# Rests of K and V formed on VectorE instead of GpSimd, and the slope product folded into the row maximum, in an attention and two-expert-layer kernel on one core

## The chip, the core and the metric

The kernel runs on one core of one Trainium2 chip. The metric is device time of that core in microseconds (us), lower is better. PE is TensorE, DVE VectorE, ACT ScalarE, POOL GpSimd, and SP the engine whose queue issues nearly all DMAs here.

## The reference

Three layers follow one another: attention with a window of 128 and a linear bias per head, a gated layer without a nonlinearity, and a routed layer of 8 experts, one per token. All inputs and the output are float32 (the weights of the gated layer arrive as float64).

```python
# attention: batch 4, 8 heads, 576 positions, 64 per head
scores = q @ k.T / sqrt(64)
scores = where((0 <= rel) & (rel < 128), scores + slopes[h] * -abs(rel), -1e9)   # slopes[h] = 2 ** -(h + 1)
scores = scores - max(scores)
attn = exp(scores); attn = attn / (sum(attn) + 1e-9)
x = attn @ v                                  # 2304 tokens x 512
# gated layer
x = ((x @ w_a) * (x @ w_b)) @ w_out           # 512 -> 1536 -> 512
# routed layer
e_idx = argmax(x @ w_gate + modality_bias[modality_id])
out[t] = gate_w[t] * (relu(x[t] @ w1[e]) @ w2[e])   # e = e_idx[t], 512 -> 1024 -> 512
```

## The kernel before

The 2304 tokens are 18 tiles of 128 rows, in seven chunks of 3, 2, 2, 3, 3, 3 and 2 tiles. For each chunk c a loop over j = 0 to 11 runs the gated layer on PE: `mm_ab` twice (tiles ps_ab, L507), the product of the two (gf, L1001 in chunk 0 and L1067 later) and its split into a rounded part and a rest (g, L1006 and L1007, later L1070 and L1071), and `mm_out` (acc, L521). Between these steps stands the attention of the next chunk: an item is one tile of one pair of heads, 72 items in all; those of chunk 0 come first, in a prologue whose order is written out by hand.

PE multiplies in a reduced form of float32 (F32R). To keep precision most operands are split in two: a part rounded by ACT, and the rest, which is the operand minus that part. For chunks 2 to 6 `a_prep_k` makes the rounded part of K on ACT (L192, from tile kr, that a DMA fills at L171) and the rest on POOL (L193, into the second half of tile kk): 20 instructions, 8 of 128x768 and 12 of 128x1024 elements. For chunks 1 to 6 `a_prep_v` does the same with V (L226 on ACT, L227 on POOL, from vr filled at L179, into vv): 24 instructions, 12 of 128x384 and 12 of 128x512. kr and vr have one buffer each, so the load of the next pair's K or V waits in SP's queue until this subtraction has read the tile.

An item's scores run so. PE makes ps_s (L244 or L248). DVE folds the two key tiles into one (`score_sel`, L256), then for each of two heads adds the mask and takes the row maximum in one instruction that also writes p (`score_max`, L262; an instruction that writes the accumulated maximum to mx follows each), then multiplies the two maxima by minus the slopes (`score_neg`, L267, 128x2 elements, from the constant tile nslope). ACT takes the exponential with that product as bias and the slope as scale (`score_exp`, L276). DVE adds 1e-9 to the sums and inverts them (L280, L285). PE turns p (L306, ps_p), ACT and DVE split it (pc, L317 and L318), POOL picks the two triangles out of pc with two affine selects (pt, L320 and L322), and PE multiplies by V (L343 in chunk 0, L378 later).

In chunk 0's loop DVE also takes apart the float64 weights: three bit operations for each half of w_a and w_b and for w_out (f64f, L438, L442, L446), and the rest of the split (wab and wo, L454). In chunk 1 and later it also does the dot products of the router (L588).

Only the prologue has a fixed order. Elsewhere the scheduler puts instructions in order by a simulated time line and priorities; preparation, scores and products of the attention have high priority. Each engine works through its own queue in that order, and an instruction that waits holds up what stands behind it.

Of the kernel before, what the change touches and what calls it, by code (L numbers as in the profile page):

```python
# [7 lines left out]
F32 = mybir.dt.float32  # L8
# [6 lines left out]
ALU = mybir.AluOpType  # L15
PSUM = bass.MemoryType.PSUM
P = 128
# [4 lines left out]
def attn_moe_moe2(ctx: ExitStack, tc, q, k, v, moe_w_a, moe_w_b, moe_w_out, modality_id,  # L22
                  w_gate, w_gate_t, modality_bias, w1, w2, out):
    nc = tc.nc
# [3 lines left out]
    H, D, S = HEADS, DM // HEADS, SEQ  # L28
# [43 lines left out]
    const = ctx.enter_context(tc.tile_pool(name="const", bufs=1))  # L72
# [43 lines left out]
    def mask_of(i):  # L116
        r = (P * i) % S
        if r == 0:
            return masks["first"]
        if S - r < P:  # L120
            assert S - r == HB
            return masks["strad"]
        if r < P:
            assert r == HB
            return masks["after"]
        return masks["base"]

    nslope = const.tile([P, H], F32, name="nslope")
    qscale = const.tile([P, NP], F32, name="qscale")
    RG = N + 3 * P  # L130
    UT = 3 * P
# [51 lines left out]
    def qq_zero(a):  # L183
        for h in range(2):
            nc.gpsimd.memset(a.qq[64 - 64 * h:128 - 64 * h, h, :], 0.0)

    def a_prep_k(a):
# [4 lines left out]
        nc.scalar.copy(out=a.kk[:, :, 0, :n], in_=a.kr[:, :, :n])  # L192
        (nc.gpsimd if KLP else nc.vector).tensor_tensor(out=a.kk[:, :, 1, :n], in0=a.kr[:, :, :n], in1=a.kk[:, :, 0, :n], op=ALU.subtract)  # L193

# [24 lines left out]
    def a_prep_v(a):  # L219
        nk = a.nt + 1  # L220
        if a.c in V32:
            a.vv = a.vr
            return
        a.vv = at.tile([P, MT + 1, 2, 2, D], F32R, tag="vv", bufs=2, name="vv")
        if a.c in V6:
            nc.scalar.copy(out=a.vv[:, :nk, 0], in_=a.vr[:, :nk])  # L226
            nc.gpsimd.tensor_tensor(out=a.vv[:, :nk, 1], in0=a.vr[:, :nk], in1=a.vv[:, :nk, 0], op=ALU.subtract)  # L227
            return
        nc.scalar.copy(out=a.vv[:, :nk, :, 0, :], in_=a.vr[:, :nk])
        nc.gpsimd.tensor_tensor(out=a.vv[:, :nk, :, 1, :], in0=a.vr[:, :nk], in1=a.vv[:, :nk, :, 0, :], op=ALU.subtract)  # L230
# [21 lines left out]
    def score_sel(it):  # L252
        a = it.a
        it.p = at.tile([P, 2, P], F32, tag="p", bufs=3, name="p")
        it.mx = at.tile([P, 8], F32, tag="mx", bufs=4, name="mx")
        nc.vector.copy_predicated(out=it.ps[:, :, P:2 * P], mask=upper.unsqueeze(1).to_broadcast([P, 2, P]), data=it.ps[:, :, 0:P])  # L256

    def score_max(it):
        a = it.a
        m = mask_of(C0[a.c] + it.t)  # L260
        for h in range(2):
            nc.vector.tensor_tensor_reduce(out=it.p[:, h, :], in0=it.ps[:, h, P:2 * P], in1=m, scale=1.0,  # L262
                                           scalar=-3.0e38, op0=ALU.add, op1=ALU.max, accum_out=it.mx[:, h:h + 1])

    def score_neg(it):
        a = it.a
        nc.vector.tensor_tensor(out=it.mx[:, 2:4], in0=it.mx[:, 0:2], in1=nslope[:, 2 * a.hp:2 * a.hp + 2], op=ALU.mult)  # L267

    def score_red(it):
        score_sel(it)  # L270
        score_max(it)
        score_neg(it)

    def score_exp(it):
        for h in range(2):
            nc.scalar.activation(out=it.p[:, h, :], in_=it.p[:, h, :], func=AF.Exp, bias=it.mx[:, 2 + h:3 + h],  # L276
                                 scale=2.0 ** -(2 * it.a.hp + h + 1), accum_out=it.mx[:, 4 + h:5 + h])

    def score_inv(it, rec=True):
        nc.vector.tensor_scalar(out=it.mx[:, 4:6], in0=it.mx[:, 4:6], scalar1=1e-9, scalar2=None, op0=ALU.add)  # L280
        if rec:
            score_rec(it)

    def score_rec(it):
        nc.vector.reciprocal(out=it.mx[:, 6:8], in_=it.mx[:, 4:6])  # L285

    def score_nrm(it):
# [44 lines left out]
    def new_xr(c):  # L332
        xr_t[c] = m1.tile([P, 2, KD, MT * P], F32R, tag="xr", bufs=1, name=f"xr{c}")
# [305 lines left out]
    @hp  # L639
    def a_loads(g):  # L640
        while pos["load"] < len(plist) and first[plist[pos["load"]]] <= g:
            c, hp = plist[pos["load"]]
            pairs[c, hp] = a_load(c, hp)
            pos["load"] += 1

    @hp
    def a_preps(g):
        while pos["prep"] < len(plist) and first[plist[pos["prep"]]] <= g:
            a = pairs[plist[pos["prep"]]]
            a_prep_k(a)  # L650
            a_prep_q(a)
            a_prep_v(a)
            pos["prep"] += 1
# [17 lines left out]
    n0 = NP * CH[0]  # L671
# [76 lines left out]
    with tc.manual_schedule():  # L748
        if WU:
            wz = m1.tile([P, 2 * P], BF16, tag="asb", bufs=2, name="wz")  # L750
            nc.vector.memset(wz.bitcast(F32), 0.0)
            wps = ps_at.tile([P, 2 * P], F32, tag="att", name="ps_w")
            for _ in range(WU):
                nc.tensor.matmul(wps, lhsT=wz[:, 0:P], rhs=wz, start=True, stop=True)
        for h in range(H):
            nc.vector.memset(qscale[64 * (h % 2):64 * (h % 2) + 64, h // 2:h // 2 + 1], 0.125 * 2.0 ** (h + 1))
        new_xr(0)
        a_loads(n0 - 1)
        qq_zero(pairs[0, 0])
        make_masks(lambda: a_preps(0))  # L760
        for h in range(H):
            nc.vector.memset(nslope[:, h:h + 1], -(2.0 ** -(h + 1)))
        for hp_ in range(1, NP):
            qq_zero(pairs[0, hp_])
        consts_load()
        wab_load(0)
        wo_load(0)
        wab_load(1)
        a_loads(n0)
        wo_load(1)  # L770
        wab_load(2)
        wab_load(3)
        for j in range(NCV):
            conv += wab_jobs(j)
            if j == 0:
                conv += wo_jobs(0)

        def st(lim, f, g, *x):
            if 0 <= g < lim:
                f(live[g], *x)  # L780

        def st_s(g):
            if 0 <= g < n0 + 2:
                c, hp, t = items[g]
                live[g] = score_mm(pairs[c, hp], t)

        def conv_step(g):
            if g >= CVS and conv:
                kd = conv[0][0]
                for _ in range(2 if kd == "s" else 1):  # L790
                    if conv and conv[0][0] == kd:
                        conv.pop(0)[1]()

        ns = n0 + 2
        for g in range(-SK, n0):
            st(n0, pt_tr, g)
            st(n0, pv_mm, g - 1)
            st(n0, pv_tr, g - 2)
            if g + SK <= n0:
                st_s(g + SK)  # L800
            r = g + SK - 1
            if r <= n0:
                st(ns, score_sel, r)
            st(n0, pv_x, g - 3, 1)
            if r <= n0:
                st(ns, score_max, r)
            st(ns, score_inv, g, False)
            if r <= n0:
                st(ns, score_neg, r)
            st(ns, score_rec, g)  # L810
            st(n0, pt_cp, g)
            st(ns, score_exp, g + 1)
            conv_step(g)
            st(n0, pv_ev, g - 1)
            st(n0, pv_x, g - 2, 0)
            if CV2 and g >= CV2:
                conv_step(g)
            if g >= -1 and (g + PRP) % CH[0] == 0 and g < n0 - CH[0]:
                a_preps(g + PRP + CH[0])
            if g == CAP - SK:  # L820
                consts_ap()
            if g == CA:
                consts_ad()
            if g == CJ:
                consts_b()
        l1, l2, i0 = (live[n0 + k] for k in (-1, -2, 0))
        pv_x(live[n0 - 3], 1)
        pv_mm(l1)
        pv_tr(l2)
        pv_ev(l1)  # L830
        mm_ab(0, 0, 0, 0)
        pv_x(l2, 0)
        pv_x(l2, 1)
        pv_tr(l1)
        pv_x(l1, 0)
        pv_x(l1, 1)
        st_s(n0 + 1)
        i1 = live[n0 + 1]
        score_red(i1)
        score_inv(i0)  # L840
        score_nrm(i0)
        pt_tr(i0)
        score_exp(i1)
        pt_cp(i0)
        score_inv(i1)
        score_nrm(i1)
# [175 lines left out]
    for c in range(NC):  # L1022
        n = CH[c] * P
        for j in range(NJ):
            if c + 1 < NC:
                b0, n1 = NP * C0[c + 1], NP * CH[c + 1]
                g = b0 + LEAD + min(n1, ((j + 1) * n1 + NJD - 1) // NJD)
            else:
                g = len(items) + 2
# [109 lines left out]
    for a, _ in zip(AE, evac_out(NC - 1)):  # L1139
# [10 lines left out]
                            op0=ALU.subtract, op1=ALU.subtract)  # L1150
# [24 lines left out]
    for o, w_, key, src in ((0, NBIG, 4, sm_f[:NS, 1:2]), (NBIG, NBIG, 4, u_[:, 13:14]),  # L1175
                            (SE, NSML, 12, sm_f[:NS, 1:2]), (SO, NSML, 12, u_[:, 14:15])):
        nc.vector.tensor_scalar(out=vt[:NS, o:o + w_], in0=iot[:NS, 0:w_], scalar1=u_[:, key:key + 1], scalar2=src,
                                op0=ALU.is_equal, op1=ALU.mult)
# [139 lines left out]
```

## Time and profile before

| | before |
|---|---|
| median of 3 runs | 883.31 us (881.21 to 883.39) |
| the profiled execution | 884.64 us, of which 882.9 us are the span from the first to the last instruction |
| busy in the span: PE | 826.9 us (94%) |
| DVE | 593.0 us (67%) |
| ACT | 435.8 us (49%) |
| POOL | 256.3 us (29%) |
| mean granted TensorE clock | 0.971 of full speed |

Busy time is the union of an engine's instructions. An instruction that the hardware holds up after it has begun counts as busy while it stands. The granted clock is 1.0 at 2.4 GHz and 0.5 at 1.2 GHz, so a mean between them is a share of either.

### The profile page before, as it was taken

How to read it: one execution, taken by the hardware profiler on the slowest of the kernel's cores; microseconds unless marked ns; L12 is line 12 of the kernel's file. 1: busy time of each engine (PE TensorE's matmuls, PEld its weight loads, DVE VectorE, ACT ScalarE, POOL GpSimd, SP SyncE). 2: the span in 40 equal slices, each digit the busy share in tenths (PEclk: the TensorE clock that was granted, in tenths of full speed). 3: DMA queues.
4: the chain of work that ended last, by engine and by line, in shares of the span. 5: the costliest groups of instructions: out<-in, count | busy, mean ns of one | idle time of the engine just before them, and what ended most of it. 6: DMA issues, size and time to landing. Idle time of an engine off the chain costs nothing.

```text
span 882.9 us, 14476 instructions
## 1 busy us (share of the span) xinstructions
PE 826.9 (94%) x4806; PEld 752.4 (85%) x4806; DVE 593.0 (67%) x1771; ACT 435.8 (49%) x1156; POOL 256.3 (29%) x289
## 2 busy tenths in 40 slices
PE   7899786989989999999999999999999999989994
PEld 5788775879888998998989999999988998978893
DVE  6999999897697779656965586358375444545420
ACT  5746464753765765656446552242245444454420
POOL 5412243342354534442334221100133120132011
PEclk9889898999999999999999999999999999998998
DMA  9993333478867455542454235547438654566201
GB/s 273 353 397 127 111 128 117 154 198 248 183 180 192 137 164 179 152 116 91 142 160 132 81 109 167 153 146 234 95 117 293 202 192 125 177 209 214 69 37 39
DMA packets 66276, 145.52 MB, mean 165 GB/s; under 512 B 11951, under 2 KB 32079, under 8 KB 66192
## 3 DMA queue, kind: packets, MB, share of 16 engines
q1 hardware_dynamic: 62576, 134.64, 50.0%
q0 software_dynamic: 3616, 9.86, 3.0%
q8 instruction: 40, 0.66, 0.3%
q14 instruction: 44, 0.36, 0.1%
HBM read 125.63 MB, written 19.11 MB: 164 GB/s over the span
## 4 chain that ended last, share of the span: by engine, by line
PE 43%; issue 24%; DVE 20%; POOL 4%; DMA 4%; ACT 3%; SPq 1%; POOLq 0%; ACTq 0%; DVEq 0%
PE ps_ab L507 24%; PE acc L521 11%; PE ps_o L378 3%; DVE junk L588 3%; DVE f64f L442 2%; DVE f64f L446 2%; POOL out L1109 2%; DMA wgt<-in_wgt 2%; POOL xg L909 2%; DVE qq L216 2%; PE ps_s L248 2%; DVE wab L454 1%; DVE p L262 1%; DVE f64f L438 1%; DVE ps_s L256 1%
## 5 line engine op out<-in xcount | busy, mean ns | idle before, releaser
L507 PE MATMUL ps_ab<-xr,wab 128*128 128x384 f32 (+1 forms) x2016 | 348.3, 321 | 21.6 <-ACT wab L453 5.9
L507 PEld LDWEIGHTS ps_ab<-xr,wab 128*128 128x128 f32 x2016 | 317.2, 192 | 35.0 <-ACT wab L453 9.7
L521 PE MATMUL acc<-wo,g 128*128 128x512 f32 x648 | 173.3, 400 | 1.0 <-DVE sc L553 0.8
L521 PEld LDWEIGHTS acc<-wo,g 128*128 128x128 f32 x648 | 116.4, 189 | 21.1 <-DVE g L1071 1.2
L1102 PE MATMUL ps_y<-w2s,h 128*128 128x512 f32 x456 | 112.2, 400 | 0.8 <-ACT h L1232 0.8
L320 POOL TENSOR_SCALAR_AFFINE_SELECT pt<-pc 128x512 fp32r<-128x512 f32 (+1 forms) x72 | 51.3, 713 | 194.7 <-DVE pc L318 111.2
L588 DVE CUSTOM_DVE_ANT_0 junk<-x,wgt 128x512 f32<-128x512 f32 x128 | 100.7, 786 | 8.2 <-DMA wgt<-in_wgt 4.4
L1119 PE MATMUL ps_h<-xT,w1s 128*128 128x384 f32 x576 | 103.2, 336 | 0.0
L1102 PEld LDWEIGHTS ps_y<-w2s,h 128*128 128x128 f32 x456 | 85.5, 191 | 18.3 <-ACT h L1232 1.0
L1119 PEld LDWEIGHTS ps_h<-xT,w1s 128*128 128x128 f32 x576 | 99.7, 188 | 1.1 <-issue 0.5
L276 ACT ACTIVATE p<-p,mx 128x128 f32<-128x128 f32 x144 | 56.7, 395 | 48.0 <-DVE mx L267 47.6
L1109 POOL DMA_INDIRECT out<-y,idx x19 | 22.3, 1171 | 166.2 <-ACT y L1108 165.0
L1070 ACT CAST g<-gf 128x256 fp32r<-128x256 f32 (+1 forms) x72 | 33.0, 459 | 62.9 <-DVE gf L1067 61.2
L193 POOL TENSOR_TENSOR kk<-kr,kk 128x1024 fp32r<-128x1024 f32 (+1 forms) x20 | 45.3, 2263 | 58.4 <-ACT kk L192 58.0
L1067 DVE TENSOR_TENSOR gf<-ps_ab,asb 128x256 f32<-128x256 f32 (+1 forms) x72 | 35.0, 486 | 40.4 <-PE ps_ab L507 31.0
L378 PE MATMUL ps_o<-pt,vv 128*128 128x256 f32 x360 | 57.2, 293 | 4.4 <-POOL pt L320 2.4
L876 DVE TENSOR_TENSOR w2s<-wr,w2s 128x1024 fp32r<-128x1024 f32 x24 | 29.3, 1225 | 43.1 <-ACT w2s L875 42.8
L378 PEld LDWEIGHTS ps_o<-pt,vv 128*128 128x128 f32 x360 | 49.9, 191 | 7.2 <-POOL pt L320 3.2
L322 POOL TENSOR_SCALAR_AFFINE_SELECT pt<-pc 128x512 fp32r<-128x512 f32 (+1 forms) x72 | 54.3, 754 | 0.0
L1063 ACT COPY asb<-ps_ab 128x256 f32<-128x256 f32 (+1 forms) x72 | 30.4, 422 | 48.4 <-PE ps_ab L507 47.1
L293 ACT ACTIVATE p<-p,mx 128x128 f32<-128x128 f32 x120 | 41.4, 394 | 25.1 <-DVE mx L285 24.2
L1123 DVE SCALAR_TENSOR_TENSOR h<-ps_h,h 128x384 fp32r<-128x384 f32 x48 | 26.6, 556 | 36.5 <-ACT h L1122 33.9
(201 smaller groups left out, 1148.8 us busy)
## 6 DMA issues: line engine op xcount, KB each, us to landing
wo<-wo_d SPq DMA_DIRECT2D x72, 512.0 KB
wr<-in_moe_w SPq DMA_DIRECT2D x56, 512.0 KB
wgt<-in_wgt SPq DMA_DIRECT2D x24, 512.0 KB
wraw<-in_moe_w_a SPq DMA_DIRECT2D x12, 512.0 KB
wraw<-in_moe_w_b SPq DMA_DIRECT2D x12, 512.0 KB
wor<-in_moe_w_out SPq DMA_DIRECT2D x12, 512.0 KB
wo_d<-wo SPq DMA_DIRECT2D x12, 512.0 KB
kr<-in_k SPq DMA_DIRECT2D x24, 256.0 KB
```

What stands on the lines that cost most here:

```text
L193: (nc.gpsimd if KLP else nc.vector).tensor_tensor(out=a.kk[:, :, 1, :n], in0=a.kr[:, :, :n], in1=a.kk[:, :, 0, :n], op=ALU.subtract)
L276: nc.scalar.activation(out=it.p[:, h, :], in_=it.p[:, h, :], func=AF.Exp, bias=it.mx[:, 2 + h:3 + h], scale=2.0 ** -(2 * it.a.hp + h + 1), ...
L293: nc.scalar.activation(out=it.p[:, h, :], in_=it.p[:, h, :], func=AF.Copy, scale=it.mx[:, 6 + h:7 + h])
L320: nc.gpsimd.affine_select(out=it.pt[:, :, 0], in_=pc, pattern=pat + [[-1, P]], base=0, channel_multiplier=1, compare_op=ALU.is_gt, fill=0.0)
L322: nc.gpsimd.affine_select(out=it.pt[:, :, 1], in_=pc, pattern=pat + [[1, P]], base=0, channel_multiplier=-1, compare_op=ALU.is_ge, fill=0.0)
L378: nc.tensor.matmul(it.po, lhsT=a.vv[:, t + b, r].rearrange("p h d -> p (h d)"), rhs=it.pt[:, :, b, s, :], start=(i == 0), stop=(i == 5))
L507: nc.tensor.matmul(ps[:, :n], lhsT=w[:, m, r, kk * P:(kk + 1) * P], rhs=xr[:, s, kk, :n], start=(idx == 0), stop=(idx == len(terms) - 1))
L521: nc.tensor.matmul(acc[c, t], lhsT=g[:, r, t * P:(t + 1) * P], rhs=w[:, s, :], start=(j == 0 and idx == 0), stop=(j == NJ - 1 and idx == 2))
L588: nc.vector.tensor_tensor_reduce(out=junk, in0=x2[:, 0:DM], in1=wgt[:, k], scale=1.0, scalar=0.0, op0=ALU.mult, op1=ALU.add, accum_out=lgr ...
L1102: nc.tensor.matmul(pss[t], lhsT=h[:, r, f, t * P:(t + 1) * P], rhs=W2[f // 2][:, s_, f % 2, :], start=(f == 0 and i == 0), stop=(f == 7 an ...
L1109: apart("out", nc.gpsimd.indirect_dma_start(out=out, out_offset=bass.IndirectOffsetOnAxis(ap=idx[:, t:t + 1], axis=0), in_=y, in_offset=No ...
L1119: nc.tensor.matmul(ps, lhsT=W1[f // 2][:, r, kk, (f % 2) * P:(f % 2 + 1) * P], rhs=xT[:, s_, kk, :], start=(kk == 0 and i == 0), stop=(kk ...
```

## The change

The rests of K (L193) and of V in chunks 1 to 6 (L227) go from POOL's queue to DVE's. `score_max` now gives each head's scale, minus its slope, and a minimum instead of a maximum, and writes into the columns of mx that held the product; p then holds the scores times minus the slope, and the exponential's scale is -1. `score_neg`, its 72 instructions, the tile nslope and its eight memsets go, and in the prologue `score_inv` is one step again.

```diff
-    KLP = 1
+    KLP = 0
...
-    nslope = const.tile([P, H], F32, name="nslope")
...
         if a.c in V6:
             nc.scalar.copy(out=a.vv[:, :nk, 0], in_=a.vr[:, :nk])
-            nc.gpsimd.tensor_tensor(out=a.vv[:, :nk, 1], in0=a.vr[:, :nk], in1=a.vv[:, :nk, 0], op=ALU.subtract)
+            nc.vector.tensor_tensor(out=a.vv[:, :nk, 1], in0=a.vr[:, :nk], in1=a.vv[:, :nk, 0], op=ALU.subtract)
             return
...
         for h in range(2):
-            nc.vector.tensor_tensor_reduce(out=it.p[:, h, :], in0=it.ps[:, h, P:2 * P], in1=m, scale=1.0,
-                                           scalar=-3.0e38, op0=ALU.add, op1=ALU.max, accum_out=it.mx[:, h:h + 1])
-
-    def score_neg(it):
-        a = it.a
-        nc.vector.tensor_tensor(out=it.mx[:, 2:4], in0=it.mx[:, 0:2], in1=nslope[:, 2 * a.hp:2 * a.hp + 2], op=ALU.mult)
+            nc.vector.tensor_tensor_reduce(out=it.p[:, h, :], in0=it.ps[:, h, P:2 * P], in1=m,
+                                           scale=-(2.0 ** -(2 * a.hp + h + 1)), scalar=3.0e38, op0=ALU.add,
+                                           op1=ALU.min, accum_out=it.mx[:, 2 + h:3 + h])
...
             nc.scalar.activation(out=it.p[:, h, :], in_=it.p[:, h, :], func=AF.Exp, bias=it.mx[:, 2 + h:3 + h],
-                                 scale=2.0 ** -(2 * it.a.hp + h + 1), accum_out=it.mx[:, 4 + h:5 + h])
+                                 scale=-1.0, accum_out=it.mx[:, 4 + h:5 + h])
...
-        for h in range(H):
-            nc.vector.memset(nslope[:, h:h + 1], -(2.0 ** -(h + 1)))
...
-            st(ns, score_inv, g, False)
-            if r <= n0:
-                st(ns, score_neg, r)
-            st(ns, score_rec, g)
+            st(ns, score_inv, g)
```

The names in the order of instructions carry buffer numbers, and the line numbers of the changed kernel are lower by 1 (up to `score_max`) to 14 (in the loop over j). In the prologue, on DVE, this is what stands between two halves of a weight's treatment before:

```order
L438 TENSOR_SCALAR f64f<-wraw_200 128x512
L350 TENSOR_SCALAR u<-ps_o,mx 128x64 x2
L724 TENSOR_SCALAR sm_i<-pidx 128x1
L726 TENSOR_SCALAR sm_i<-pidx 128x1
L727 CAST sm_f<-sm_i 128x2
L728 TENSOR_SCALAR sm_f<-sm_f 128x1
L729 TENSOR_SCALAR sm_f<-sm_f 128x1
L256 COPY_PREDICATED ps_s<-upper,ps_s 128x2x128
```

The same place on DVE in the changed kernel:

```order
L429 TENSOR_SCALAR f64f<-wraw_191 128x512
L341 TENSOR_SCALAR u<-ps_o,mx 128x64 x2
L715 TENSOR_SCALAR sm_i<-pidx 128x1
L717 TENSOR_SCALAR sm_i<-pidx 128x1
L192 TENSOR_TENSOR kk<-kr_0_743,kk 128x2x384
L718 CAST sm_f<-sm_i 128x2
L719 TENSOR_SCALAR sm_f<-sm_f 128x1
L720 TENSOR_SCALAR sm_f<-sm_f 128x1
L255 COPY_PREDICATED ps_s<-upper,ps_s 128x2x128
```

The first rest of K (L192 of the changed kernel) now stands between small constants, ahead of the next item's score_sel (L255).

In the middle of chunk 0's loop, on DVE, the seventh j before: g is the rest of the gated product, wab_1327 and wo the rests of weights, qq the rescaled Q of the second pair of chunk 2.

```order
L256 COPY_PREDICATED ps_s<-upper,ps_s 128x2x128
L1007 TENSOR_TENSOR g<-gf,g 128x384
L454 TENSOR_TENSOR wab_1327<-f64f,wab_1327 128x512 x2
L446 SCALAR_TENSOR_TENSOR f64f<-wor,f64f 128x512
L262 ISA p,mx<-ps_s,m_strad 128x128
L262 ISA mx 128x1
L262 ISA p,mx<-ps_s,m_strad 128x128
L262 ISA mx 128x1
L216 SCALAR_TENSOR_TENSOR qq<-qr_1_776,qscale,qq 64x256
L438 TENSOR_SCALAR f64f<-wraw_1158 128x512
L216 SCALAR_TENSOR_TENSOR qq<-qr_1_776,qscale,qq 64x256
```

What stands on DVE around the same two qq in the changed kernel, one j earlier:

```order
L255 COPY_PREDICATED ps_s<-upper,ps_s 128x2x128
L192 TENSOR_TENSOR kk<-kr_1_750,kk 128x2x384
L215 SCALAR_TENSOR_TENSOR qq<-qr_1_753,qscale,qq 64x256 x2
L437 SCALAR_TENSOR_TENSOR f64f<-wor,f64f 128x512
L993 TENSOR_TENSOR g<-gf,g 128x384
L445 TENSOR_TENSOR wab_1212<-f64f,wab_1212 128x512
L261 ISA p,mx<-ps_s,m_strad 128x128
L261 ISA mx 128x1
L261 ISA p,mx<-ps_s,m_strad 128x128
L261 ISA mx 128x1
L445 TENSOR_TENSOR wab_1212<-f64f,wab_1212 128x512
L226 TENSOR_TENSOR vv<-vr_0_748,vv 128x3x128
```

The pair's rest of K and its two qq moved ahead of g (L993) and of the weights' rests (L445), and a rest of V follows them.

## Rows read from the trace of the kernel before

**Rows 1.** Windows of three stretches: length; busy us of PE, PEld, DVE, ACT, POOL; clock; DMA

```profile
47.00:178.00 131.00, 113.96 (x588) 101.45 (x587) 123.29 (x285) 74.55 (x206) 40.29 (x40) 0.91 0.48 169
178.00:282.00 104.00, 95.56 (x675) 88.06 (x676) 85.29 (x309) 55.61 (x179) 40.66 (x39) 0.98 0.77 200
282.00:530.00 248.00, 244.42 (x1476) 227.90 (x1476) 176.96 (x587) 145.94 (x447) 95.50 (x97) 1.00 0.46 134
```

**Rows 2.** PE's waits from 47 to 178 us: total us, times, longest us

```profile
PE ps_ab L507 <- ACT wab L453: 5.9, 4, 2.4
PE ps_ab L507 <- DVE wab L454: 5.8, 4, 3.1
```

**Rows 3.** Timeline at 266 to 271 us: start, duration, engine, what

```profile
266.18 2.83 POOL L193 TENSOR_TENSOR kk<-kr,kk 128x1024 fp32r<-128x1024 f32 x1
...
266.69 2.33 DVE L267 TENSOR_TENSOR mx<-mx,nslope 128x2 f32<-128x2 f32 x1
...
269.05 0.61 DVE L216 SCALAR_TENSOR_TENSOR qq<-qr,qscale,qq 64x384 fp32r<-64x384 f32 x1
...
270.51 1.88 PE L507 MATMUL ps_ab<-xr,wab 128*128 128x256 f32 x9 [2.02 <-ACT asb L1063]
```

**Rows 4.** Line L267: shortest, median and longest duration in ns

```profile
L267 DVE TENSOR_TENSOR mx<-mx,nslope x72: 147/161/2330, 7.4 to 523.8; 128x2 f32<-128x2 f32 x72
```

**Rows 5.** Timeline at 61 to 65 us, a rest of V

```profile
61.87 1.76 DVE L438 TENSOR_SCALAR f64f<-wraw 128x512 uint32<-128x512 uint32 x2
...
62.17 1.17 POOL L227 TENSOR_TENSOR vv<-vr,vv 128x384 fp32r<-128x384 f32 x1
...
64.72 0.42 DVE L438 TENSOR_SCALAR f64f<-wor 128x512 uint32<-128x512 uint32 x1
```

**Rows 6.** Timeline at 143 to 148 us, a rest of K

```profile
143.58 2.11 POOL L193 TENSOR_TENSOR kk<-kr,kk 128x768 fp32r<-128x768 f32 x1
...
143.99 2.24 DVE L446 SCALAR_TENSOR_TENSOR f64f<-wraw,f64f 128x512 uint32<-128x512 uint32 x1
...
147.36 0.68 DVE L446 SCALAR_TENSOR_TENSOR f64f<-wraw,f64f 128x512 uint32<-128x512 uint32 x1
```

**Rows 7.** Timeline at 173 to 178 us, the last two rests before 178 us

```profile
173.80 3.63 DVE L216 SCALAR_TENSOR_TENSOR qq<-qr,qscale,qq 64x384 fp32r<-64x384 f32 x2 [0.36 <-ACT qq L215]
175.84 1.17 POOL L227 TENSOR_TENSOR vv<-vr,vv 128x384 fp32r<-128x384 f32 x1
```

**Rows 8.** Windows of L193 alone on POOL: length, busy us (instructions), clock, DMA

```profile
47.00:178.00 131.00, 8.76 (x4) 0.91 0.48 169
178.00:282.00 104.00, 10.00 (x4) 0.98 0.77 200
```

**Rows 9.** Window of L227 alone on POOL

```profile
47.00:178.00 131.00, 8.84 (x7) 0.91 0.48 169
```

**Rows 10.** Window of L267 alone on DVE

```profile
47.00:178.00 131.00, 3.28 (x13) 0.91 0.48 169
```

**Rows 11.** Timeline at 9 to 10 us, L267 and the instruction behind it

```profile
9.57 0.16 DVE L267 TENSOR_TENSOR mx<-mx,nslope 128x2 f32<-128x2 f32 x1
...
9.65 0.17 DVE L285 RECIPROCAL mx<-mx 128x2 f32<-128x2 f32 x1
```

**Rows 12.** Groups by line on DVE, whole span: busy us, mean ns

```profile
L876 DVE TENSOR_TENSOR w1s<-wr,w1s 128x1024 fp32r<-128x1024 f32 x28 | 34.3, 1225 | 20.6 <-ACT w1s L875 20.1 <-issue 0.4
...
L262 DVE CUSTOM_DVE_ANT_0 p<-ps_s,m_base 128x128 f32<-128x128 f32 x96 | 23.9, 285 | 0.7
```

**Rows 13.** Line L454: shortest, median and longest duration in ns

```profile
L454 DVE TENSOR_TENSOR wab<-f64f,wab x24: 673/686/1116, 31.9 to 160.6; 128x512 fp32r<-128x512 f32 x24
```

**Rows 14.** POOL's waits, whole span: total us, times, longest us

```profile
POOL kk L193 <- ACT kk L192: 58.0, 13, 12.7
POOL vv L227 <- ACT vv L226: 24.3, 8, 7.4
```

**Rows 15.** Groups by line on POOL, whole span

```profile
L322 POOL TENSOR_SCALAR_AFFINE_SELECT pt<-pc 128x512 fp32r<-128x512 f32 x60 | 48.7, 812 | 0.0
```

**Rows 16.** Waits for loads of K, whole span

```profile
ACT kk L192 <- DMA kr<-in_k: 2.8, 3, 1.9
```

More of the change, by code (lines that the diff above doesn't have):

```diff
@@ L271, in score_red @@
         score_max(it)
-        score_neg(it)
     def score_exp(it):
@@ L276, in score_exp, with score_inv @@
             nc.scalar.activation(out=it.p[:, h, :], in_=it.p[:, h, :], func=AF.Exp, bias=it.mx[:, 2 + h:3 + h],
-                                 scale=2.0 ** -(2 * it.a.hp + h + 1), accum_out=it.mx[:, 4 + h:5 + h])
-    def score_inv(it, rec=True):
+                                 scale=-1.0, accum_out=it.mx[:, 4 + h:5 + h])
+    def score_inv(it):
         nc.vector.tensor_scalar(out=it.mx[:, 4:6], in0=it.mx[:, 4:6], scalar1=1e-9, scalar2=None, op0=ALU.add)
-        if rec:
-            score_rec(it)
-    def score_rec(it):
         nc.vector.reciprocal(out=it.mx[:, 6:8], in_=it.mx[:, 4:6])
```

## The prediction, made before the changed kernel ran

> **What bounds the kernel now.** I read the windows by stage first, with stages cut where chunk 0's loop (47 to 178 us), chunk 1's (178 to 282 us, with the start of chunk 2) and the later attention (282 to 530 us) run. From 47 to 178 us DVE is busy for 123.29 of 131 us and PE for 113.96, at a mean clock of 0.91; from 282 to 530 us PE is busy for 244.42 of 248 us at full clock [rows 1]. So chunk 0's loop is bound by DVE, which takes the weights apart there, and the rest of the program by PE. PE's waits say the same: in chunk 0's loop the longest are for wab, which ACT and DVE split (5.9 and 5.8 us) [rows 2]. From 178 to 282 us PE stands idle for 104 - 95.56 = 8.4 us, from 282 to 530 us for 3.6 us [rows 1]; that is all that any edit of the attention can give back there, and behind 530 us nothing of this change runs.
>
> What DVE's busy time is made of shows only in the timeline. At 266.69 us L267, a product of 128x2 elements, takes 2.33 us; its median is 161 ns [rows 3, 4]. It ends at 269.02 us, and POOL's rest of K, begun at 266.18 us, ends at 269.01 us. PE then waits 2.02 us for an ACT copy that stood in ACT's queue behind that item's exponential [rows 3]. The same is seen wherever a rest runs on POOL: two L438 take 1.76 us beside a rest of V, where one alone takes 0.42 us; L446 takes 2.24 us beside a rest of K, alone 0.68 us; two L216 take 3.63 us, alone 0.61 us each [rows 3, 5 to 7]. DVE stands until POOL's subtraction ends. The reader should see that POOL's long instructions are paid on DVE, the engine that bounds chunk 0.
>
> The Trainium skill says why (SBUF — State Buffer, "Who interferes with whom"): VectorE and GpSimd share a pair of ports under an exclusive lock, and a VectorE instruction with two SBUF inputs waits for a GpSimd instruction that reads SBUF, to its end. By that rule all the 8.76 + 8.84 = 17.6 us of rests on POOL in chunk 0's loop could stand on DVE, where the rows that I summed below show 12.8; the sum would then be 4.8 us better.
>
> **The change, part by part, in chunk 0's loop.** Four rests of K (8.76 us on POOL) and seven of V (8.84 us) run there [rows 8, 9]. Beside each of the eleven I took from the DVE instructions that it overlaps what they last beyond the shortest of their form: 1.0 us at the first (two L438 at 62.17 us, which overlap a little), 1.56 us at the rest of K at 143.58 us, 3.63 - 2 x 0.61 = 2.4 us at the last two together [rows 3, 5 to 7]; over all eleven 12.8 us. That goes.
>
> L267 goes too: 13 instructions, 3.28 us of busy time [rows 10]. Alone, one costs less than its 161 ns: L267 begins at 9.57 us and the reciprocal behind it at 9.65 [rows 11]. I take 0.08 us each, 1.0 us; the nearest bounds are 0 (the reciprocal would then wait for the addition ahead of it instead) and 0.16. Its time beyond the median, 3.28 - 13 x 0.16 = 1.2 us, was waiting for POOL's selects, which stay; half of it, 0.6 us, will move to a neighbour. So 1.6 us go.
>
> What comes: the same subtractions on DVE. No row shows them; the nearest are subtractions of the same kind, 1225 ns for 128x1024 and at the shortest 673 ns for 128x512 [rows 12, 13], which is 1.08 ns per element. So 0.95 us for 128x768, 0.53 for 128x384, 0.67 and 1.23 for the larger ones. In chunk 0's loop 4 x 0.95 + 7 x 0.53 = 7.5 us. They too can meet a select: L454, of the same kind, has a median of 686 ns and a longest of 1116 [rows 13], so I add 5%, 0.4 us. Bounds: 7.5 us, and 11 x 0.44 = 4.9 us more if each met a select as badly as that longest.
>
> The sum is 12.8 + 1.6 - 7.9 = 6.5 us less on the engine that bounds the stage, by the bounds from about 1 (each rest meets a select, L267 was free) to 12 (all 17.6 us of POOL's time stood on DVE). PE can follow: it has 131 - 113.96 = 17 us of idle time there and runs below full clock [rows 1].
>
> **The other stages.** Ahead of 47 us one rest of K and one of V come to DVE, 0.95 + 0.53 us, and 13 L267 of 0.08 us go, with about as much waiting as chunk 0's share for one rest of V; I take 0. From 178 to 282 us four rests of K hold POOL for 10.00 us [rows 8]. DVE has 18.7 us of idle time there [rows 1], so it isn't the sum of its work that counts but single stalls that PE sees, such as the 2.02 us above. I put most of PE's 8.4 us down to such stalls, or to pt waiting in POOL's queue behind a rest. The rest of K then stands on DVE for 1.23 us in place of a stall of up to 2.3: half comes back, 4 us (bounds 0 and 8.4). From 282 to 530 us PE idles for 3.6 us in all; I take 1 (bounds 0 and 3.6).
>
> The loads of the next K and V into kr and vr now wait for DVE instead of POOL. ACT waited for K's landing for only 2.8 us in the whole span [rows 16], so I cost this at nothing; without that cover a late load would hold ACT's queue, with g and asb behind it, for up to the 1.9 us of the longest such wait.
>
> Total: 6.5 + 0 + 4 + 1 = 11.5 us. The profiled execution took 884.64 us, so 873.1 us; it lies 1.3 us above the median of 883.31, so against that **871.8 us**.
>
> **Rivals.**
> *Slower: DVE waits for ACT's casts.* A rest needs its rounded part. POOL waited 58.0 us for the casts of K and 24.3 us for those of V [rows 14], and it had nothing else to do. On DVE such a wait holds g, the weights' rests and the next scores. The order speaks for it: the pair's rest of K and its qq now stand ahead of g and of wab in chunk 0. If the 19 rests from 47 to 282 us wait as long as POOL waited on the mean for a cast of V (24.3 / 8 = 3 us) in one case of three, that is 19 us; less 11.5 gives 7.5 us slower, 891 us. It decides from a mean wait of 0.6 us per rest. Against it: ACT is busy for 74.55 of 131 us where DVE is for 123.29 [rows 1], so DVE is the one that comes late, and the casts should be done by then.
>
> *No change: the lock moves on.* By the Trainium skill's rule the moved subtractions, with two SBUF inputs, wait for POOL's selects, that read SBUF. In rows: a select lasts 812 ns [rows 15]. If every one of the 19 rests up to 282 us waited for half a select, and selects for rests as long again ahead of PE's product with V, 19 x 0.4 = 7.7 us go back, and with the gain beyond 282 us lost too the time is 881 us; the reordered queues of chunks 0 to 5, which move waits of PE about, can take the remainder. Against it: L454's median is within 13 ns of its shortest [rows 13].
>
> *More: PE's waits feed on each other.* If the DVE work saved lies just ahead of wab and g, PE's waits for wab (11.7 us) [rows 2], the 8.4 us of the next stage and 3.6 us behind it all go: 23.7 us, 858 us median. DVE's remaining work in chunk 0, 123.29 - 6.5 = 116.8 us, allows 131 - 116.8 = 14.2 us there. Against it: PE would have to find every operand ready.
>
> *The fold costs.* No row shows the maximum's instruction with a scale other than 1 or with a minimum. If it took twice its 285 ns [rows 12], the 26 of chunk 0's loop would eat 7.4 us of the 11.5: 879 us. I give this little, since it does the same three steps per element.
>
> **Chances.** The forecast (864 to 880 us) 0.50, more gain 0.16, no change or the fold's cost (880 to 886 us) 0.15, slower 0.19. A difference of under 0.3%, 2.6 us, can't be told from none here. Of the forecast and the greater gain together, 0.66, nearly all is faster than 880.7 us, as is a part of the case at 881: faster 0.69, same 0.12, slower 0.19. The range reaches from 859 us, short of the greatest gain, to 888 us, into the slower case: what lies outside is about 0.08 on either side. The forecast's own range is 864 to 880 us.
>
> **What would show it.** Right: DVE's L446, L216 and L588 near the shortest of their forms; the loop of chunk 0 about 124 us long; DVE's busy time down by 15 to 30 us in the span though 44 subtractions came; POOL's down by 77. Wrong: DVE idle ahead of the moved subtractions with ACT's casts as releaser; L454 and the rests lasting up to a select longer; the first gf of chunk 1 no earlier than 178 us; or PE's waits from 178 us on as long as before but for other names.

## The result and the profile after

The changed kernel takes 862.18 us (median of 4 runs, 860.9 to 863.43) beside 882.26 us for the kernel before on the same chip: ratio 0.9766, interval 0.975 to 0.9782, so 20.1 us faster. The forecast was 871.8 us, 11.5 us faster. The gain is 1.75 times that: the time lies in the outer range (859 to 888 us), but 1.8 us below the forecast's own (864 to 880 us).

First the windows by stage, cut where PE begins the gated layer and where the last split of g of chunk 0 and of chunk 6 ends. The lines give the stretch, its length, busy time of PE, PEld, DVE, ACT and POOL with instruction counts, the granted clock, and the DMA's share and GB/s. Before:

```profile
46.90:170.10 123.20, 107.06 (x540) 95.16 (x541) 117.59 (x276) 67.58 (x188) 36.68 (x37) 0.91 0.48 167
170.10:639.90 469.80, 456.89 (x2885) 424.09 (x2884) 328.34 (x1120) 238.55 (x717) 149.74 (x149) 1.00 0.55 156
639.90:882.90 243.00, 227.05 (x1191) 203.81 (x1189) 108.57 (x184) 102.04 (x159) 46.93 (x41) 0.97 0.46 152
```

After:

```profile
45.60:163.70 118.10, 102.25 (x540) 89.97 (x541) 111.73 (x273) 68.42 (x188) 28.10 (x28) 0.97 0.52 180
163.70:619.30 455.60, 452.18 (x2884) 420.76 (x2883) 313.23 (x1106) 239.74 (x718) 92.78 (x116) 1.00 0.54 161
619.30:861.50 242.20, 226.96 (x1191) 203.53 (x1189) 108.47 (x184) 102.30 (x159) 46.11 (x41) 0.97 0.46 153
```

Of the 21.4 us by which the span of the profiled execution shrank, the prologue gave 1.3, chunk 0's loop 5.1, chunks 1 to 6 14.2 and what follows 0.8. In chunks 1 to 6 PE's idle time fell from 469.80 - 456.89 = 12.9 us to 455.60 - 452.18 = 3.4 us, and its busy time by 4.7 us. In chunk 0's loop PE's idle time stayed (16.1 and 15.9 us); its busy time fell by 4.8 us, at a granted clock of 0.97 in place of 0.91 (what that means is taken up with the prediction).

PE's waits in chunks 1 to 6 (total us, times, longest us), before:

```profile
PE ps_ab L507 <- DVE gf L1067: 4.5, 5, 1.8
PE ps_ab L507 <- ACT asb L1063: 3.3, 3, 2.0
PE ps_o L378 <- POOL pt L320: 2.0, 2, 1.3
PE ps_o L378 <- DVE mx L262: 1.5, 1, 1.5
...
```

After, all that there are:

```profile
PE ps_ab L498 <- ACT asb L1049: 2.1, 3, 1.4
PE acc L512 <- DMA wo<-wo_d: 1.0, 1, 1.0
```

Waits for DVE and for POOL, 9.6 us before with the three shorter ones left out here, are gone; of those for ACT 1.2 us are. In chunk 0's loop the two waits for wab of [rows 2], 11.7 us in all, are down to 0.9 us, and others have come up, so that PE's idle time there is as long as before:

```profile
PE ps_p L297 <- ACT p L284: 5.0, 3, 2.7
PE ps_s L247 <- ACT xf L375: 2.4, 2, 1.3
PE acc L512 <- DVE wo L445: 2.0, 1, 2.0
...
PE ps_ab L498 <- DVE wab L445: 0.9, 2, 0.6
```

DVE's groups by line and form (count, then busy us, mean ns, idle before) tell where its time went. Before:

```profile
L588 DVE CUSTOM_DVE_ANT_0 junk<-x,wgt 128x512 f32<-128x512 f32 x128 | 100.7, 786 | 8.2 <-DMA wgt<-in_wgt 4.4 <-ACT x L602 2.1
L267 DVE TENSOR_TENSOR mx<-mx,nslope 128x2 f32<-128x2 f32 x72 | 28.0, 389 | 1.0
L216 DVE SCALAR_TENSOR_TENSOR qq<-qr,qscale,qq 64x384 fp32r<-64x384 f32 x24 | 24.5, 1021 | 2.9 <-ACT qq L215 2.2
```

After (L579 was L588, L215 was L216, L261 was L262; L192 and L226 are the moved rests):

```profile
L579 DVE CUSTOM_DVE_ANT_0 junk<-x,wgt 128x512 f32<-128x512 f32 x128 | 91.6, 715 | 8.5 <-DMA wgt<-in_wgt 4.9 <-ACT x L593 2.0
L261 DVE CUSTOM_DVE_ANT_0 p<-ps_s,m_base 128x128 f32<-128x128 f32 x96 | 23.8, 284 | 0.5
L215 DVE SCALAR_TENSOR_TENSOR qq<-qr,qscale,qq 64x384 fp32r<-64x384 f32 x24 | 15.0, 625 | 0.8
L192 DVE TENSOR_TENSOR kk<-kr,kk 128x1024 fp32r<-128x1024 f32 x12 | 14.6, 1220 | 0.2
L226 DVE TENSOR_TENSOR vv<-vr,vv 128x512 fp32r<-128x512 f32 x12 | 10.9, 905 | 3.9 <-ACT vv L225 3.9
L226 DVE TENSOR_TENSOR vv<-vr,vv 128x384 fp32r<-128x384 f32 x12 | 7.0, 585 | 3.6 <-ACT vv L225 3.6
L192 DVE TENSOR_TENSOR kk<-kr,kk 128x768 fp32r<-128x768 f32 x8 | 7.7, 964 | 0.1
```

The rests cost DVE 14.6 + 10.9 + 7.0 + 7.7 = 40.2 us, L267's 28.0 us are gone, and DVE as a whole is busy for 570.5 us, 22.5 less: so its other instructions lost 22.5 + 40.2 - 28.0 = 34.7 us, nearly all of it time in which they stood. The reader should see it in L215: its mean of 625 ns is near the 0.61 us of one that stands alone [rows 3].

### The profile page after: what moved, and what is told of

Read it like the earlier page. It is cut to its first block, busy times and chain, and to the rows that moved or that the text cites. A ratio compares the mean times of both kernels' runs of the same rounds, so it can differ in the third digit from the quotient of the medians.

```text
span 861.5 us, 14391 instructions
## 1 busy us (share of the span) xinstructions
PE 815.5 (95%) x4806; PEld 742.1 (86%) x4806; DVE 570.5 (66%) x1735; ACT 438.0 (51%) x1156; POOL 187.0 (22%) x245
## 4 chain that ended last, share of the span: by engine, by line
PE 49%; issue 23%; DVE 10%; DMA 7%; POOL 4%; ACT 4%; SPq 1%; POOLq 0%; ACTq 0%; DVEq 0%
PE ps_ab L498 27%; PE acc L512 13%; PE ps_o L369 4%; PE ps_s L247 2%; POOL out L1095 2%; POOL xg L895 2%; DVE f64f L433 1%; DVE f64f L437 1%; DMA qr<-in_q 1%; PE ps_p L297 1%; DMA wraw<-in_moe_w_b 1%; DMA vr<-in_v 1%; DMA kr<-in_k 1%; DVE wab L445 1%; DVE f64f L429 1%
## 5 line engine op out<-in xcount | busy, mean ns | idle before, releaser
L498 PE MATMUL ps_ab<-xr,wab 128*128 128x384 f32 (+1 forms) x2016 | 340.1, 317 | 7.1 <-ACT asb L1049 2.1
L498 PEld LDWEIGHTS ps_ab<-xr,wab 128*128 128x128 f32 x2016 | 309.6, 189 | 19.3 <-ACT wab L444 4.9
L311 POOL TENSOR_SCALAR_AFFINE_SELECT pt<-pc 128x512 fp32r<-128x512 f32 (+1 forms) x72 | 57.4, 797 | 324.0 <-DVE pc L309 211.6
L579 DVE CUSTOM_DVE_ANT_0 junk<-x,wgt 128x512 f32<-128x512 f32 x128 | 91.6, 715 | 8.5 <-DMA wgt<-in_wgt 4.9
L271 ACT ACTIVATE p<-p,mx 128x128 f32<-128x128 f32 x144 | 56.7, 395 | 30.5 <-DVE mx L261 29.8
L1095 POOL DMA_INDIRECT out<-y,idx x19 | 22.2, 1170 | 166.8 <-ACT y L1094 165.6
L313 POOL TENSOR_SCALAR_AFFINE_SELECT pt<-pc 128x512 fp32r<-128x512 f32 (+1 forms) x72 | 56.7, 788 | 0.0
L1108 ACT ACTIVATE h<-ps_h 128x384 fp32r<-128x384 f32 x48 | 23.5, 492 | 55.5 <-PE ps_h L1105 55.5
L255 DVE COPY_PREDICATED ps_s<-upper,ps_s 128x256 f32<-128x256 uint8 x72 | 30.9, 429 | 26.1 <-PE ps_s L247 17.7
```

Source lines behind the costliest of these rows:

```text
L311: nc.gpsimd.affine_select(out=it.pt[:, :, 0], in_=pc, pattern=pat + [[-1, P]], base=0, channel_multiplier=1, compare_op=ALU.is_gt, fill=0.0)
L313: nc.gpsimd.affine_select(out=it.pt[:, :, 1], in_=pc, pattern=pat + [[1, P]], base=0, channel_multiplier=-1, compare_op=ALU.is_ge, fill=0.0)
L498: nc.tensor.matmul(ps[:, :n], lhsT=w[:, m, r, kk * P:(kk + 1) * P], rhs=xr[:, s, kk, :n], start=(idx == 0), stop=(idx == len(terms) - 1))
L579: nc.vector.tensor_tensor_reduce(out=junk, in0=x2[:, 0:DM], in1=wgt[:, k], scale=1.0, scalar=0.0, op0=ALU.mult, op1=ALU.add, accum_out=lgr ...
L1095: apart("out", nc.gpsimd.indirect_dma_start(out=out, out_offset=bass.IndirectOffsetOnAxis(ap=idx[:, t:t + 1], axis=0), in_=y, in_offset=No ...
```

## The experiments

All times are medians, and each ratio is taken beside the kernel before on the same chip. The rounds ran on several chips, where the kernel before had medians of 881.3 to 882.65 us; between rounds the ratios are the surer comparison. The stages are those of the windows above, of one profiled execution each, so differences of 1 to 3 us between them are weak evidence. "Standing" is worked out from the trace: for each form of DVE instruction, what its instructions last beyond the duration that a tenth of them stay under, summed over the span (differences under 40 ns left out).

| kernel | us | ratio (interval) | prologue and chunk 0 | chunks 1 to 6 | DVE busy in chunk 0's loop / its length | standing |
|---|---|---|---|---|---|---|
| before | 882.3 | 1 | 170.1 | 469.8 | 117.6 / 123.2 | 69 |
| V's rests | 873.73 | 0.9896 (0.9869 to 0.9923) | 162.2 | 466.5 | 112.8 / 114.7 | 54 |
| K's rests | 869.93 | 0.9857 (0.9839 to 0.9874) | 164.8 | 462.6 | 112.6 / 117.5 | 35 |
| both rests | 870.67 | 0.9869 (0.984 to 0.9897) | 163.8 | 461.4 | 113.0 / 116.5 | 23 |
| fold | 872.32 | 0.9885 (0.9863 to 0.9907) | 164.4 | 463.6 | 115.1 / 119.2 | 61 |
| fold, V's rests | 876.85 | 0.9934 (0.9909 to 0.996) | 164.5 | 464.9 | 113.2 / 118.3 | 53 |
| fold, K's rests | 867.84 | 0.9838 (0.9815 to 0.9861) | 160.9 | 460.9 | 113.0 / 116.1 | 33 |
| changed kernel | 862.18 | 0.9766 (0.975 to 0.9782) | 163.7 | 455.6 | 111.7 / 118.1 | 20 |
| + POOL subtracts too | 890.11 | 1.0095 (1.0068 to 1.0122) | 176.8 | 469.3 | 123.8 / 130.6 | 65 |
| + POOL fills | 863.45 | 0.9795 (0.9771 to 0.982) | 163.2 | 455.5 | 112.8 / 116.7 | 28 |
| fold, product kept | 877.23 | 0.996 (0.9942 to 0.9979) | 167.7 | 464.6 | 117.4 / 121.1 | 67 |
| changed, product kept | 866.9 | 0.9833 (0.9807 to 0.9858) | 163.3 | 458.3 | 113.5 / 116.1 | 25 |
| before, q first | 883.76 | 1.0003 (0.9983 to 1.0023) | 169.2 | 473.3 | 116.7 / 122.5 | 60 |
| changed, q first | 862.17 | 0.9776 (0.9748 to 0.9804) | 162.5 | 456.3 | 112.0 / 116.4 | 22 |

**The fold alone.** The changed kernel with both rests back on POOL:

```diff
-    KLP = 0
+    KLP = 1
...
-            nc.vector.tensor_tensor(out=a.vv[:, :nk, 1], ...)
+            nc.gpsimd.tensor_tensor(out=a.vv[:, :nk, 1], ...)
```

> The fold alone: the row maximum's instruction takes the slope's product in, and the rests of K and V stay on GpSimd. Theory A (GpSimd's rests hold VectorE, and taking them off GpSimd is the gain): 1 to 5 us of the 20.1 us come back, 877 to 881 us, and GpSimd's rests still last 2.0 to 2.8 us with VectorE instructions of the same length beside them. Theory B (the gain is the score's shorter chain: the product L267 was the instruction that stood longest behind the rests, and ACT's exponential behind it): 10 to 15 us, 867 to 872 us. Theory C (the scheduler's other order is the gain, whatever the reason for it): no prediction for this run alone, but the parts don't add up.

872.32 us, so the fold alone brings about 10 us: at the upper edge of theory B's range, and far from theory A's.

**The rests alone.** The kernel before with `KLP = 0` and V's subtraction on VectorE; L267 stays.

> The rests of K and V on VectorE alone, with the product L267 kept. Theory A: 15 to 19 us of the 20.1 us, 863 to 867 us; L267's longest falls from 2.33 us to under 1 us, since only GpSimd's selects can hold it. Theory B: 5 to 10 us, 872 to 877 us. Theory C: with e1, the gains of the two parts miss the sum of 20.1 us by more than 5 us.

870.67 us, about 11 us, between the ranges of theories A and B. The two halves add up to the whole here. The fold was worth much more than the prediction gave it.

**The fold with V's rests, and with K's.** The changed kernel with `KLP = 1`, and with V's subtraction alone back on POOL.

> The changed kernel with the rest of K alone back on GpSimd (20 instructions, 45 us there). Theory A: it loses 8 to 13 us against the changed kernel, 870 to 875 us, K's share by time on GpSimd being 45 of 77 us. Theory B: under 5 us, 863 to 867 us. Theory C: anything, and not in proportion to e4.

> The changed kernel with the rest of V alone back on GpSimd (24 instructions, 32 us there). Theory A: it loses 5 to 9 us against the changed kernel, 867 to 871 us, less than K. Theory B: under 4 us. Theory C: anything, more than K among it.

876.85 us, slower than any theory gave, and 867.84 us, as theory A had it. Beside the fold alone V's move is a loss of 4.5 us while K's rests are on POOL, and a gain of 5.7 us once they are gone. That does not add up, and the last four runs below take it up.

**POOL subtracts too.** Is it the shared access that matters, or where the rests stand? The changed kernel, with POOL forming each rest as well, into a tile that nobody reads:

```diff
+        nc.gpsimd.tensor_tensor(out=scr, in0=a.kr[:, :, :3 * P], in1=a.kk[:, :, 0, :3 * P], op=ALU.subtract)
```

(and the same for V).

> The changed kernel with one thing added: at each of the 44 places POOL also forms the rest of K or V, into a scratch tile that nobody reads; the rests that are used still come from VectorE. The lock theory (a VectorE instruction with two SBUF inputs stands until a POOL instruction that reads SBUF ends): the hold is back, VectorE's time beyond the shortest of each form goes from about 20 us to over 50, and about the half of the gain that the rests brought goes: 870 to 876 us, though the product of 128x2 that was its worst victim is no longer there. The order theory (what pays is only where the rests stand and how the scheduler lays the rest around them): the order is nearly that of the changed kernel, so 862 to 866 us.

890.11 us, 28 us more than the changed kernel. More than either theory gave: it is slower than the kernel before.

**POOL fills.** In place of that subtraction a cast of one element and three fills, writes only:

```diff
+        nc.gpsimd.tensor_copy(out=scr[:, 0, 0:1], in_=a.kk[:, 0, 0, 0:1])
+        for _ in range(3):
+            nc.gpsimd.memset(scr, 0.0)
```

> The changed kernel with POOL kept busy at the same 44 places for about as long, but by filling a scratch tile with a constant (three fills and a cast of one element that ties them to the place), so that POOL writes SBUF and does not read it. The lock theory: no hold, VectorE's time beyond the shortest forms stays at about 20 us, 861 to 866 us. The rival, that what hurts is POOL's queue (the selects of pt stand behind a long instruction), not what it reads: as much slower as the run with the subtraction, 870 to 876 us.

863.45 us, within 1.3 us of the changed kernel, though POOL is busier here than with the subtraction (283.5 us of the span, beside 263.9). The timelines show the difference on one rest of K and the two parts of qq behind it (start, duration, engine, what). With POOL's subtraction:

```profile
316.61 1.22 DVE L193 TENSOR_TENSOR kk<-kr,kk 128x1024 fp32r<-128x1024 f32 x1
316.70 2.83 POOL L194 TENSOR_TENSOR scr<-kr,kk 128x768 bf16<-128x768 f32 x1 [0.85 <-POOL scr L230]
...
317.86 2.74 DVE L217 SCALAR_TENSOR_TENSOR qq<-qr,qscale,qq 64x384 fp32r<-64x384 f32 x2
```

With POOL's fills:

```profile
295.88 1.22 DVE L193 TENSOR_TENSOR kk<-kr,kk 128x1024 fp32r<-128x1024 f32 x1
...
296.06 2.33 POOL L196 MEMSET scr<- 128x768 bf16 x3
...
297.13 1.26 DVE L219 SCALAR_TENSOR_TENSOR qq<-qr,qscale,qq 64x384 fp32r<-64x384 f32 x2
```

The two parts of qq take 2.74 us beside a POOL instruction that reads and 1.26 us beside fills. Over the span DVE stands for 65 us in the one kernel, 45 of them beside the added subtractions, and for 28 in the other, 4 of them beside the fills. The rule of the Trainium skill that the prediction named (SBUF — State Buffer, "Who interferes with whom") holds in both halves: two SBUF inputs contend with POOL's reads and not with its writes. The rival, POOL's queue, falls: in the kernel with fills its selects stand behind work of like length (2.33 and 2.83 us here), and from chunk 0's loop to the end of chunk 6 PE never waits for POOL in the kernel with subtractions. Two things besides differ between the pair. The added subtraction also reads kr and vr, so their next load waits for it: ACT waited 4.2 us for loads of K there and 1.2 us beside the fills, and PE's waits in that stretch name no load of K or V. And the scheduler laid about 15% of PE's matmuls in another order; the last two runs show what such a shift is worth by itself.

**The product kept, off the chain.** What of the fold pays: the product's time on DVE, or that the exponential no longer waits for it? The fold, with L267 still formed at its place from the new columns into two that nobody reads, once with the rests on POOL, once in the changed kernel:

```diff
-        nc.vector.tensor_tensor(out=it.mx[:, 2:4], in0=it.mx[:, 0:2], in1=nslope[...], op=ALU.mult)
+        nc.vector.tensor_tensor(out=it.mx[:, 0:2], in0=it.mx[:, 2:4], in1=nslope[...], op=ALU.mult)
```

> The kernel before with the multiplication folded into the maximum's operation, but the product of 128x2 still formed at its old place, into two columns that nobody reads; the rests stay on POOL. If the 9.6 us of the fold alone (872.3 us) came from the product's time and its stalls on VectorE, nothing is gained: 879 to 884 us. If they came from the exponential, which now starts at the maximum and not behind the product: 870 to 875 us.

> The changed kernel (rests on VectorE, fold) with the product of 128x2 still formed at its old place, into two columns that nobody reads. If the product costs by its time and stalls on VectorE, the time is that of the rests alone: 868 to 872 us. If it costs by standing ahead of the exponential, it is that of the changed kernel: 861 to 865 us.

877.23 and 866.9 us: both fall between. By the ratios, the product's time and standing on DVE are worth 0.9960 - 0.9885 = 0.75% or 6.6 us with the rests on POOL and 0.9833 - 0.9766 = 0.67% or 5.9 us without (by the medians 4.9 and 4.7 us, which compare different chips). The earlier exponential is worth 0.4% or 3.5 us beside the kernel before, and 0.9869 - 0.9833 = 0.36% or 3.2 us beside the rests alone (the intervals of these last two overlap a little). So both count, by the ratios the product's time on DVE more. Where in the program each acts is not shown. With the rests on POOL, the product kept but off the chain brings 469.8 - 464.6 = 5.2 of the fold's 6.2 us in chunks 1 to 6; but in the changed kernel taking the product away altogether brings 458.3 - 455.6 = 2.7 us there and nothing ahead of them, and the first pair's spans differ by 8.0 us where the ratio gives 3.5.

**V alone, K alone, without the fold.** The kernel before with V's subtraction on VectorE, and with `KLP = 0`.

> The kernel before with the rests of V alone on VectorE; the fold is not made and the rests of K stay on POOL. The runs so far have V's move at a loss of 4.5 us where K's rests stay on POOL and at a gain of 5.7 us where they are on VectorE, both with the fold. If that belongs to the pairing (V's rests on VectorE stand for K's on POOL, and VectorE has more to do), it is the same without the fold: 884 to 889 us. If it is the scheduler's new order of that one kernel, V's move is worth its share of the hold here, 876 to 881 us.

> The kernel before with the rests of K alone on VectorE, nothing else. VectorE's time beyond the shortest forms should fall from 69 us to about 40, K's rests being behind 30 of it. If the parts add, K is worth two thirds of the 11 us of both rests, 873 to 876 us. With the pairing as in the runs with the fold (K's move alone 4.5 us, 14.7 when V has moved): 875 to 879 us, and the run with V alone above 884.

873.73 and 869.93 us, both better than any number expected. V's move without the fold is a gain of 8 us, so the loss beside the fold does not belong to the pairing with K alone. Either move alone brings nearly as much as both.

**The order alone.** One pair of calls swapped, in the kernel before and in the changed one; the instructions are the same. In the traces a fifth of PE's matmuls in the one kernel and a quarter in the other stand outside the order that both versions share, more than the tenth that the text below names, and as many as one of the edits moves (16 to 27%):

```diff
-            a_prep_k(a)
             a_prep_q(a)
+            a_prep_k(a)
```

> The kernel before with one pair of calls swapped: a pair's q is prepared ahead of its K. Every instruction is the same; only the order in which the scheduler lays them moves (about a tenth of PE's rows stand elsewhere). It measures what a re-laid order alone is worth, since the moves of K, of V and the fold, taken in every combination, do not add up (V's move is worth +9 us to -4 us by what else has moved). If the parts act by their own prices, and the order is worth little: 880 to 884 us, the same as before. If a re-laid order alone is worth several us: outside 878 to 886.

> The changed kernel with the same swap: a pair's q prepared ahead of its K, all instructions the same. If the order is worth little: 860 to 864 us. If a re-laid order alone is worth several us: outside 858 to 866; by what this and the run on the kernel before show, the differences between the combinations are read.

883.76 us (1.0003, 0.9983 to 1.0023) and 862.17 us. This re-laid order was worth nothing in either kernel, which speaks against order alone as the cause of what fails to add up; one swap in two kernels does not rule it out in the others. In the kernel before, it took 9 us of standing away (69 to 60) and the time stayed: how long DVE stands is not by itself what the kernel pays.

## Why the prediction was right, and where its sizes were off

**The mechanism: right, and shown.** DVE's instructions with two SBUF inputs stood until POOL's rests ended. Before, 50.8 of the 69 us of standing lie beside a rest on POOL and 17.9 beside a select; after, 18.7 of 20 lie beside a select. The runs with POOL subtracting and POOL filling differ by 26.7 us, with the hold back in the one and not in the other. L438 of [rows 5], which takes one input, is outside the rule as the prediction told it; the last section has a case of its kind. DVE's busy time fell by 22.5 us (15 to 30 were named), POOL's by 69.3 where 77 were named: its selects now last longer (mean of the second 859 ns, [rows 15] 812).

**Chunk 0's loop: right.** 5.1 us where 6.5 were forecast; DVE's busy time there fell by 5.9 us. Two of the forecast's eleven rests, those at 173 to 177 us, stand behind the end of this loop as the windows above cut it, before and after. For the nine that stand in it the forecast's own terms give 12.8 - 2.4 = 10.4 us of standing, 1.6 of L267 and 6.3 for the subtractions on DVE, 5.7 us in sum (its lowest sum for all eleven, "about 1", is 12.8 - 7.5 - 4.9 = 0.4). Measured: the rests cost 6.65 us, L267 gave back its 3.1 us, so 5.9 + 6.65 - 3.1 = 9.4 us of other standing went. The forecast's stage ended at 178 us, where the first gf of chunk 1 stands (177.8 us; 166.8 in the changed kernel). By that cut the stage went from 130.9 to 121.2 us, 9.7 less where 6.5 were forecast, and two rests and eight other instructions on DVE moved out of it.

A higher clock is not what shortened the loop. With K's rests alone it ran at 0.91, as before, and still took 117.5 us:

```profile
47.30:164.80 117.50, 104.03 (x518) 92.78 (x519) 112.60 (x278) 66.38 (x184) 25.39 (x30) 0.91 0.50 172
```

That DVE bounds the loop fits all kernels: its length is DVE's work and 2 to 7 us more, from 112.8 us of work in 114.7 to 123.8 in 130.6. But the parts don't add there. Any one of the three edits takes DVE from 117.6 to between 112.6 and 115.1 us, and the other two find little left. A likely reason, not tested, is that a rest moved to DVE costs there what its removal from POOL no longer gives. So prologue and loop together lose 5.3 to 9.2 us in each of the seven kernels.

**Ahead of 47 us: 0 forecast, 1.3 us measured**, and 1.7 with the fold alone.

**Chunks 1 to 6: the term that was mis-sized.** The step was "half comes back, 4 us" for 178 to 282 us, and 1 us for 282 to 530: 5 us forecast (5.8 with the two rests above), 14.2 measured. Cut at the first gf of chunk 1, where the forecast cut it, the stretch went from 462.1 to 452.5 us, 9.6 less: still about twice the forecast. Two things were missing.

The first is the fold. The prediction priced L267 in chunk 0's loop alone, from its window there [rows 10], and gave the 47 in the later chunks nothing since DVE has idle time there. The same view of the stages, for that line:

```profile
0.00:46.90 46.90, 3.01 (x13) 0.88 0.98 319
46.90:170.10 123.20, 3.12 (x12) 0.91 0.48 167
170.10:639.90 469.80, 21.91 (x47) 1.00 0.55 156
```

Of DVE's 28.0 us in L267, 21.9 lie in the chunks that were given none, 47 x 0.161 = 7.6 us of it work by the median of [rows 4] and 14.3 us standing. Each stands ahead of an exponential in ACT's queue, with asb behind it, for which PE waits; that is the stall of 2.02 us in [rows 3], which the prediction read and counted with K's rest alone. In chunks 1 to 6 the fold alone brings 6.2 us, K's rests 7.2 and V's 3.3: 16.7 together by their sum, 14.2 measured. That is not a sign that the parts add: of pairs, the fold and V's rests bring 4.9 of 9.5 us, the fold and K's rests 8.9 of 13.4, both rests 8.4 of 10.5, and cut at the first gf of chunk 1 all three bring 9.6 of 16.4.

The second is the share of PE's idle time. The windows put the ceiling at 8.4 + 3.6 = 12.0 us, and half of the larger part was taken. In fact 9.5 of 12.9 us came back, nearly all of it waits for DVE and POOL. And the ceiling was not one: PE's busy time fell by 4.7 us beside it. In the kernel before, the stretch of the 2.02 us wait ran at a lower clock:

```profile
248.00:290.00 42.00, 39.54 (x279) 36.95 (x280) 33.49 (x127) 24.09 (x78) 21.88 (x21) 0.96 0.69 190
```

A mean of 0.96 over 42 us is about 3.4 us at 1.2 GHz, and so about 1.7 us lost. It followed the wait, which ended at 270.51 us: from 268 to 270 us the granted clock was 1.00, from 270 to 272 us 0.76, from 272 to 274 us 0.50, and from 276 us 1.00 again. Neither is in the changed kernel, where PE's longest wait in these chunks is 1.4 us and the clock is 1.00. Where the other 3 us lie was not settled: the matmuls of ps_ab last a little less in the trace (L507's mean 313 ns in these chunks, L498's 311; 3.0 us in all), but those of acc are busy for 1.4 us more.

**The rivals.** *DVE waits for ACT's casts*: it does, for 3.9 + 3.6 us ahead of V's rests and 0.3 us ahead of K's, where POOL had waited 82.3 us; 7.8 us over 44 rests is 0.2 us each, under the 0.6 from which that rival would have decided. *The lock moves on*: in part. V's larger rest has a mean of 905 ns and a shortest of 679. One place in the changed kernel's timeline:

```profile
244.63 0.97 POOL L311 TENSOR_SCALAR_AFFINE_SELECT pt<-pc 128x512 fp32r<-128x512 f32 x1 [4.36 <-PE acc L512]
...
245.03 1.12 DVE L226 TENSOR_TENSOR vv<-vr,vv 128x512 fp32r<-128x512 f32 x1
245.56 1.09 POOL L313 TENSOR_SCALAR_AFFINE_SELECT pt<-pc 128x512 fp32r<-128x512 f32 x1
...
246.07 1.12 DVE L579 CUSTOM_DVE_ANT_0 junk<-x,wgt 128x512 f32<-128x512 f32 x1
```

The rest, begun beside one select, ends late, and the next select and the dot product behind it each take their turn. But that is 12 x 0.23 = 2.7 us in the span. What stands beside the selects alone is about as much after, 18.7 us, as before, 17.9. *More gain*: its 23.7 us off 883.31 make 859.6 us and not the 858 that it names. The measured time lies much nearer to it than to the forecast; PE's waits did go almost whole in chunks 1 to 6, as it said, but not in chunk 0's loop. That rival had a chance of 0.16, and the forecast, which had 0.50, was too small. *The fold costs*: no, its maximum takes 284 ns, beside 285 in [rows 12]. The loads of K and V show in none of PE's waits.

**What stays open.** Beside the fold and with K's rests on POOL, moving V's rests made the kernel 4.5 us slower (872.32 and 876.85 us), where without the fold it gained 8. In the profiled executions 1.3 us of it lie in chunks 1 to 6, and 1.6 in the last stage, where none of these instructions runs. The order alone moved nothing in the two kernels tried; in this one it was not tried. Why the parts don't add, in the loop and behind it, is open too.

## What to carry to other kernels

In this kernel instructions that read two SBUF operands on VectorE paid for what POOL read at the time, the smallest of them too. Before giving such a line the price of its median, sum its busy time beyond count times median, over all stages, and look at what is queued behind it. Whether a hold comes from shared access or from queue order can be told apart by replacing POOL's reading instruction with one that only writes. And don't add up the gains of the parts of one change, nor read them off stages cut at one place alone: here the two halves added up, pairs of the three edits fell far short, and another cut moved 4.6 us from one stage to the next.

## What the runs showed of the hardware

A fill on POOL can hold one kind of DVE instruction. In the kernel with fills, this addition of 1e-9 to 128x2 elements stands until POOL's fills end, at 223.51 + 2.33 = 225.84 us:

```profile
223.44 1.26 DVE L219 SCALAR_TENSOR_TENSOR qq<-qr,qscale,qq 64x384 fp32r<-64x384 f32 x2
223.51 2.33 POOL L196 MEMSET scr<- 128x768 bf16 x3
...
225.07 0.79 DVE L282 TENSOR_SCALAR mx<-mx 128x2 f32<-128x2 f32 x1
```

Its median is 169 ns. Three more of the 72, of 775 to 793 ns, also end within 0.03 us of a fill's end. The two parts of qq beside the same fills, with two SBUF inputs each, took 1.26 us, about as long as two alone (0.61 us each in [rows 3]). The Trainium skill (SBUF — State Buffer, "Who interferes with whom") says that a tensor_scalar can enter a mode that contends with GpSimd for the shared pair of ports; the trace agrees, with these 0.79 us.

The hold works in both directions. POOL's subtraction at 316.70 us, which began 0.09 us after DVE's rest, took 2.83 us where the shortest of its form took 1.83. Means of whole groups do not show it as plainly: the two affine selects went from 763 and 812 ns before to 862 and 859 in the changed kernel, but only to 769 and 821 with both rests on DVE and the product kept on the chain, so the added subtractions alone do not account for that rise.
